# Six 0/1 patterns built on GpSimd, and a mean subtracted in one operation, in a gated window-attention decode step

## The chip, the cores and the metric

The kernel runs on one core of one Trainium2 chip. A core has five engines that run their own instruction streams: TensorE (PE: matrix products), VectorE (DVE: element by element, sums and 32x32 transposes), ScalarE (ACT: functions and copies), GpSimd (POOL) and SyncE (SP, which here only issues transfers). Sixteen DMA engines move data between the chip's memory (HBM) and the on-chip memory SBUF; matrix products go into a third memory, PSUM. Engines wait for each other by semaphores.

The metric is device time in microseconds (us), the median of several runs. The profile is one further execution, recorded by the hardware profiler; its span goes from the first to the last instruction.

## The reference

One decode step, batch 2, one new token, all numbers 32-bit floats. With `xn = layernorm(x)`:

```python
def _A_ref(x, k_cache, v_cache, wq, wo):          # x: [2, 1, 512]
    W = min(4096, max(256, Sk // 4))              # the last 4096 of 32768 positions
    q = heads_of(x @ wq)                          # 32 heads of 128
    k = repeat(k_cache[:, :, Sk - W:, :], 4)      # 8 key heads, each for 4 query heads
    v = repeat(v_cache[:, :, Sk - W:, :], 4)
    p = softmax(q @ k^T * 128 ** -0.5)
    return rows_of(p @ v) @ wo                    # wo: [4096, 512]

def _B_ref(x, w_in, w_sp, b_sp, w_out):           # w_in: [512, 1792], w_out: [896, 512]
    z = gelu(x @ w_in)
    z1, z2 = z[..., :896], layernorm(z[..., 896:])
    g = w_sp * z2 + b_sp
    return (z1 * g) @ w_out

out = x + _A_ref(xn, ...) * silu(_B_ref(xn, ...))
```

## The kernel before, in words

**Data.** A ring of four SBUF slots (`ring`) takes every large load. The loads are queued in this order, all on SyncE's DMA queue: `w_in` (slot 0), `w_out` (slot 1), `wq` (slots 2 and 3), then the units of keys and values, then `wo` in pieces. A unit is the window of two key heads of one batch row, 4096 KB of keys and as much of values; there are eight. Their order is k0, k1, v0, k2, v1, and so on to k7, v6, v7. A load is issued when its slot is free, and `advance` (line 92) is called where the program has finished with a slot. So k0 follows the products of z (slot 0, line 268), k1 the products of y (slot 1, line 321), v0 and k2 the products of q (slots 2 and 3, line 343), v1 the last transpose of k0, and so on.

**Order.** VectorE, ScalarE, TensorE and SyncE are called through a wrapper (`InOrder`, line 27), and execute in the order in which the program is written. GpSimd is called directly; before the change it makes the identity matrix and clears some tiles (lines 184 to 201), all at the start.

**Opening.** VectorE sums the identity into `rowm` (128x32, a one where row mod 32 is the column) and `grpm`, then normalizes x (lines 218 to 227). TensorE turns it, and VectorE copies it into `xnT` (line 231). Then VectorE builds the constant patterns of lines 233 to 257, all from `rowm`, `rowr`, `diag` and `am`, which are sums over columns of `rowm`:
- `same` (128x128, ones where the rows agree mod 32) is the weight of the product `rp`, which adds up the masked q (line 355);
- `same_r` (128x128) is that of the products `mo`, for the maximum and the sum of the softmax (lines 395 and 416);
- `sel` (128x56) selects the rows of a unit in `collect` (line 451), and `place` (128x131) places the heads in `gather` (line 464);
- `add_dq` (128x131) adds the four shares of a score in `add_shares` (line 386);
- `negm` (128x2, 0 or -1e30) is part of the bias of the exponential, `nb` (line 399); `spot` masks the maxima (line 392).

**z and its mean.** When `w_in` is there, 32 products make z (line 264), VectorE transposes it, and works out gelu on 128x28 values. For the layernorm of z's second half, a product with ones sums over the rows, VectorE sums the 7 columns of each batch row into `mean`, and two VectorE operations scale it and subtract it:

```python
mean_over_rows(mean, z2, "mean_ps")
dve.tensor_scalar_mul(mean, mean, 1.0 / FH)
dve.tensor_sub(z2, z2, ap(mean, 0, per_b))
dve.tensor_mul(w2, z2, z2)
mean_over_rows(var, w2, "var_ps")
```

The tile `mean` is later written anew by `rsqrt`. The result goes to `hT`, 14 products with `w_out` make y (line 318), and the gate follows. Then q is made, turned and spread (lines 334 to 358).

**Units.** For each unit, VectorE transposes the keys in four parts (`turn`, tile `kt`), TensorE makes scores (`shares`, `add_shares`), VectorE, TensorE and ScalarE make the softmax of the unit before, and TensorE multiplies it with the values (`values`, tile `acc`). At the end the products with `wo` are added up, multiplied by the gate, added to x and stored (lines 515 to 536).

Of the kernel before, what the change touches and what calls it, by code (L numbers as in the profile page):

```python
# [11 lines left out]
ALU = mybir.AluOpType  # L12
AX = mybir.AxisListType

P = 128
HQ, DH = 32, 128
G = 4
EPS = 1e-5
BIG = 1e30


def ap(t, offset, dims):

    return bass.AP(tensor=t.tensor, offset=t.offset + offset, ap=[list(t.ap[0])] + [list(d) for d in dims])
# [18 lines left out]
def kernel(  # L43
# [13 lines left out]
    nc = tc.nc  # L57
    pe, dve, act, sp = (InOrder(tc, e) for e in (nc.tensor, nc.vector, nc.scalar, nc.sync))
# [5 lines left out]
    FH = F // 2  # L64
# [7 lines left out]
    NCH = J // JC  # L72
# [28 lines left out]
    def const(name, *shape):  # L101
        return cst.tile([P, *shape], F32, tag=name, name=name)
# [92 lines left out]
    sel = const("sel", 56)  # L195
    nc.gpsimd.memset(sel, 0.0)
    place = const("place", 3 + P)
# [5 lines left out]
    rowm = const("rowm", 32)  # L203
# [27 lines left out]
    dve.tensor_copy(xnT[:, :, :B], pt)  # L231

    same = const("same", G, 32)
    dve.tensor_copy(same, ap(rowm, 0, [[0, G], [1, 32]]))
    same = same.rearrange("p g c -> p (g c)")
    rowr = const("rowr", 8)
    dve.tensor_reduce(rowr, rowm.rearrange("p (r m) -> p r m", m=NCH), axis=AX.X, op=ALU.add)
    same_r = const("same_r", G, 8, NCH)
    dve.tensor_copy(same_r, ap(rowr, 0, [[0, G], [1, 8], [0, NCH]]))
    same_r = same_r.rearrange("p g r m -> p (g r m)")  # L240
    diag = const("diag", NCH)
    dve.tensor_reduce(diag, rowm.rearrange("p (r m) -> p m r", m=NCH), axis=AX.X, op=ALU.add)
    dve.tensor_copy(sel[:, 24:32], rowr)
    dve.tensor_copy(place[:, 3 : 3 + P : 4], rowm)
    for a in range(2):
        dve.tensor_copy(
            ap(add_dq, NCH - 1 + 16 * a, [[32, G], [4, REP]]),
            rowm[:, 16 * a : 16 * a + 16].rearrange("p (g h) -> p g h", g=G),
        )
    am = const("am", 2)  # L250
    dve.tensor_reduce(am, rowm.rearrange("p (a x) -> p a x", a=2), axis=AX.X, op=ALU.add)
    negm = const("negm", 2)
    dve.tensor_scalar(negm, am, -1.0, BIG, op0=ALU.add, op1=ALU.mult)
    spot = const("spot", 2, G, NCH)
    for a in range(2):
        dve.tensor_mul(spot[:, a], ap(grpm, 0, [[1, G], [0, NCH]]), ap(diag, 0, [[0, G], [1, NCH]]))
# [33 lines left out]
    z1, z2, w2 = zT[:, 0], zT[:, 1], uu[:, 0]  # L290
    mean, var = const("mean", B), const("var", B)

    def mean_over_rows(dst, src, name):
        pm = bank(name, "mo")[:, : FT * B]
        pe.matmul(pm, ones, src.rearrange("p j b -> p (j b)"), start=True, stop=True)
        dve.reduce_sum(dst, pm.rearrange("p (j b) -> p b j", b=B), axis=AX.X)

    per_b = [[0, FT], [1, B]]
    mean_over_rows(mean, z2, "mean_ps")
    dve.tensor_scalar_mul(mean, mean, 1.0 / FH)  # L300
    dve.tensor_sub(z2, z2, ap(mean, 0, per_b))
    dve.tensor_mul(w2, z2, z2)
    mean_over_rows(var, w2, "var_ps")
    dve.tensor_scalar(var, var, 1.0 / FH, EPS, op0=ALU.mult, op1=ALU.add)
# [260 lines left out]
```

## Time and profile before

| | before |
|---|---|
| median of 3 runs | 218.9 us (218.65 to 219.15) |
| the profiled execution's own time | 218.71 us |
| its span | 216.9 us |
| VectorE instructions, busy | 176, 108.5 us |
| GpSimd instructions, busy | 14, 2.6 us |
| TensorE matrix products, busy | 866, 153.2 us |
| read from HBM | 89.40 MB |

How to read it: a row of the timeline is the start in us, the duration in us, the engine, the line of the code, the operation, the tile written, `<-`, the tiles read, their shapes, and how many instructions are merged in the row. In square brackets stands how long the engine stood idle before, and what ended that. All operations that go through the wrapper carry the wrapper's line, L37, so they are told apart by their tiles. `SPq` is SyncE's queue: its rows are issues of transfers. A row of the windows gives, for a stretch A:B of the span, its length, then the busy time of each engine with the number of instructions, the granted clock of TensorE, the mean busy share of the sixteen DMA engines, and GB/s. A row of the groups gives the busy time of all instructions of one kind, and after the comma the mean of one in ns. The chain of waits goes back from the last instruction to what released it, again and again. Packets and matrix products are recorded with modelled ends, so that in a short stretch a share can be over 1.

### The profile page before, as it was taken

To read this page: it belongs to the slowest core of one execution; us is meant where nothing else is said; L and a number is where in the kernel's file an instruction comes from. 1 tells how busy PE (TensorE), PEld (TensorE's weight loads), DVE (VectorE), ACT (ScalarE), POOL (GpSimd) and SP (SyncE) were. 2 spreads that over 40 slices of the span, in tenths; PEclk is the share of its full clock that TensorE was granted. 3 is DMA by queue.
4 is the path that set the end of the run, shared out by engine and by line. 5 is a ranking of instruction groups with operands and counts; after the bars stand their busy time and mean duration, and the time that the engine had idled before them with its cause. 6 is when DMAs were issued, how large, how long until landed. Compare 5 with 4: busy or idle time off the path is not lost.

```text
span 216.9 us, 2230 instructions
## 1 busy us (share of the span) xinstructions
PE 153.2 (71%) x866; PEld 42.9 (20%) x866; DVE 108.5 (50%) x176; ACT 44.0 (20%) x109; POOL 2.6 (1%) x14
## 2 busy tenths in 40 slices
PE   0173163943987995994997698469959958997761
PEld 0121110200221221221221121322212211232210
DVE  2505411069959369538806942594578089321001
ACT  4003310000222133042113203120421331242010
POOL 4000000000000000000000000000000000000000
PEclk9997575896796997998599799857996996999997
DMA  7998897999999999999999999999999999999980
GB/s 255 423 532 387 387 545 320 468 393 477 393 459 411 447 420 441 429 417 447 405 452 411 453 411 450 417 441 429 429 435 432 435 417 441 417 444 411 407 321 3
DMA packets 3790, 89.54 MB, mean 413 GB/s; under 512 B 434, under 2 KB 450, under 8 KB 964
## 3 DMA queue, kind: packets, MB, share of 16 engines
q1 hardware_dynamic: 3772, 89.40, 96.3%
q8 instruction: 7, 0.11, 0.2%
q14 instruction: 3, 0.02, 0.0%
q10 hardware_dynamic: 8, 0.00, 0.0%
HBM read 89.40 MB, written 0.00 MB: 412 GB/s over the span
## 4 chain that ended last, share of the span: by engine, by line
DMA 70%; PE 17%; DVE 10%; issue 1%; SPq 0%; DVEq 0%
DMA ring<-in_A_k_cache_dram 34%; DMA ring<-in_A_wo_dram 20%; DMA ring<-in_A_wq_dram 16%; DVE kt L37 8%; PE q_ps L37 4%; PE acc L37 4%; PE sh L37 4%; PE s L37 3%; PE mo L37 1%; PE oT L37 0%; PE col L37 0%; SPq L37 0%; DVE res L37 0%; DVE pT L37 0%; DVE m L37 0%
## 5 line engine op out<-in xcount | busy, mean ns | idle before, releaser
L37 DVE STREAM_TRANSPOSE kt<-ring 128x2048 f32<-128x2048 f32 x32 | 72.5, 2294 | 35.6 <-DMA ring<-in_A_k_cache_dram 25.8
L37 PE MATMUL sh<-kt,qbd 128*32 128x512 f32 x256 | 41.8, 706 | 14.8 <-DVE kt L37 14.8
L37 ACT ACTIVATE shs<-sh 128x512 f32<-128x512 f32 x32 | 19.1, 597 | 119.6 <-PE sh L37 119.6
L37 PE MATMUL s<-shs,add_dq 128*128 128x512 f32 x64 | 40.7, 742 | 0.0
L37 PE MATMUL acc<-ring,pT 128*32 128x512 f32 x256 | 31.9, 639 | 0.2 <-DVE pT L37 0.2
L37 PEld LDWEIGHTS s<-shs,add_dq 128*128 128x128 f32 x64 | 11.2, 218 | 29.9 <-issue 25.5
L37 PEld LDWEIGHTS sh<-kt,qbd 128*32 128x32 f32 x256 | 6.6, 113 | 34.6 <-issue 21.0
L37 PEld LDWEIGHTS acc<-ring,pT 128*32 128x32 f32 x256 | 7.7, 117 | 26.1 <-issue 18.3
L37 PE MATMUL q_ps<-ring,xnT 128*32 128x512 f32 x64 | 8.9, 721 | 4.8 <-DMA ring<-in_A_wq_dram 4.8
L37 PE MATMUL mo<-l,same_r 128*128 128x2 f32 x16 | 3.3, 274 | 10.6 <-ACT p L37 10.6
L37 ACT ACTIVATE o<-acc,wd 128x128 f32<-128x128 f32 x32 | 9.1, 373 | 3.4 <-PE acc L37 3.4
L37 ACT ACTIVATE p<-s,nb 128x256 f32<-128x256 f32 x16 | 7.6, 489 | 7.2 <-DVE nb L37 6.9
L37 PE MATMUL part<-ring,oT 128*32 128x512 f32 x56 | 6.6, 597 | 3.3 <-DMA ring<-in_A_wo_dram 3.3
L37 DVE TENSOR_REDUCE m<-s 128x2 f32<-128x512 f32 x8 | 5.4, 676 | 6.8 <-PE s L37 6.8
L37 PE MATMUL col<-o,sel 128*32 128x512 f32 x16 | 8.3, 601 | 0.4 <-ACT o L37 0.4
L37 PE MATMUL z<-ring,xnT 128*32 128x448 f32 x32 | 5.1, 810 | 4.2 <-DMA ring<-in_B_w_in_dram 4.2
L37 DVE STREAM_TRANSPOSE qT<-q_ps 128x512 f32<-128x512 f32 x2 | 1.4, 717 | 10.8 <-PE q_ps L37 10.7
L37 DVE TENSOR_TENSOR res<-so,gate 128x128 f32<-128x128 f32 x1 | 0.3, 292 | 11.7 <-PE so L37 11.7
L37 DVE STREAM_TRANSPOSE pT<-p 128x512 f32<-128x512 f32 x8 | 5.4, 673 | 1.2 <-ACT p L37 1.2
L37 PE MATMUL y<-ring,hT 128*32 128x512 f32 x14 | 3.2, 969 | 3.8 <-issue 3.8
L37 PE MATMUL xnT_ps<-ident,xn 2*128 2x2 f32 x4 | 0.6, 252 | 7.3 <-DVE xn L37 7.3
L37 ACT ACT_TABLE_LOAD x4 | 5.1, 1283 | 1.9 <-issue 1.9
(106 smaller groups left out, 64.4 us busy)
## 6 DMA issues: line engine op xcount, KB each, us to landing
ring<-in_A_k_cache_dram SPq DMA_DIRECT2D x8, 4096.0 KB, 28.2
ring<-in_A_v_cache_dram SPq DMA_DIRECT2D x8, 4096.0 KB, 30.8
ring<-in_A_wo_dram SPq DMA_DIRECT2D x1, 4096.0 KB, 33.2
ring<-in_B_w_in_dram SPq DMA_DIRECT2D x1, 3584.0 KB, 11.2
ring<-in_A_wo_dram SPq DMA_DIRECT2D x1, 2048.0 KB, 27.4
ring<-in_B_w_out_dram SPq DMA_DIRECT2D x1, 1792.0 KB, 15.1
ring<-in_A_wo_dram SPq DMA_DIRECT2D x1, 1024.0 KB
ring<-in_A_wo_dram SPq DMA_DIRECT2D x4, 256.0 KB, 17.5
```

The lines of the kernel that those rows point to most:

```text
L37: return self.tc.keep_in_program_order(call(*args, **kwargs))
```

## The change

Seven VectorE instructions that build six patterns (`same`, `same_r`, `sel`, `place`, `add_dq` in two halves, `negm`) are issued on GpSimd. The sums over columns that they read (`rowm`, `rowr`, `am`), and `diag` and `spot`, stay on VectorE. GpSimd also clears `sel`, `place` and `add_dq`, as before. In z's layernorm, the scaling of the sum and the subtraction become one operation, z2 = sum x (-1/896) + z2; the tile `mean` then holds the sum until `rsqrt` writes it.

```diff
     same = const("same", G, 32)
-    dve.tensor_copy(same, ap(rowm, 0, [[0, G], [1, 32]]))
+    nc.gpsimd.tensor_copy(same, ap(rowm, 0, [[0, G], [1, 32]]))
...
-    dve.tensor_copy(same_r, ap(rowr, 0, [[0, G], [1, 8], [0, NCH]]))
+    nc.gpsimd.tensor_copy(same_r, ap(rowr, 0, [[0, G], [1, 8], [0, NCH]]))
...
-    dve.tensor_copy(sel[:, 24:32], rowr)
-    dve.tensor_copy(place[:, 3 : 3 + P : 4], rowm)
+    nc.gpsimd.tensor_copy(sel[:, 24:32], rowr)
+    nc.gpsimd.tensor_copy(place[:, 3 : 3 + P : 4], rowm)
     for a in range(2):
-        dve.tensor_copy(
+        nc.gpsimd.tensor_copy(
             ap(add_dq, NCH - 1 + 16 * a, [[32, G], [4, REP]]),
...
-    dve.tensor_scalar(negm, am, -1.0, BIG, op0=ALU.add, op1=ALU.mult)
+    nc.gpsimd.tensor_scalar(negm, am, -1.0, BIG, op0=ALU.add, op1=ALU.mult)
...
     mean_over_rows(mean, z2, "mean_ps")
-    dve.tensor_scalar_mul(mean, mean, 1.0 / FH)
-    dve.tensor_sub(z2, z2, ap(mean, 0, per_b))
+    dve.scalar_tensor_tensor(z2, ap(mean, 0, per_b), -1.0 / FH, z2, op0=ALU.mult, op1=ALU.add)
     dve.tensor_mul(w2, z2, z2)
```

## The prediction

> **What bounds the kernel now.** I read the first page from the top: the span, the busy shares, then the DMA queue and the chain.
>
> ```profile
> span 216.9 us, 2230 instructions
> PE 153.2 (71%) x866; PEld 42.9 (20%) x866; DVE 108.5 (50%) x176; ACT 44.0 (20%) x109; POOL 2.6 (1%) x14
> ...
> q1 hardware_dynamic: 3772, 89.40, 96.3%
> ...
> DMA 70%; PE 17%; DVE 10%; issue 1%; SPq 0%; DVEq 0%
> ```
>
> VectorE is busy half of the span, GpSimd 1%, and one DMA queue 96.3%: 89.40 MB pass through it. The chain of waits gives DMA 70% and still leaves 10% to VectorE and 17% to TensorE. Those two shares say that some load was issued only when VectorE or TensorE had freed its slot. They do not say that the DMA engines stood idle until then. That is a question for the stretches of time, for which I ended each stretch at an issue of SyncE's queue.
>
> ```profile
> core 0: us, PE busy (x) PEld busy (x) DVE busy (x) ACT busy (x) POOL busy (x), PEclk, DMA share, GB/s
> 1.60:30.30 28.70, 10.45 (x56) 3.99 (x56) 9.51 (x48) 6.72 (x11) 1.58 (x6) 0.82 1.06 446
> 1.60:58.60 57.00, 26.76 (x157) 7.72 (x157) 24.55 (x71) 8.81 (x14) 1.58 (x6) 0.79 1.00 427
> 1.60:72.40 70.80, 37.94 (x208) 10.75 (x212) 35.76 (x83) 12.22 (x22) 1.58 (x6) 0.81 1.01 432
> 1.60:202.30 200.70, 144.90 (x770) 40.26 (x770) 107.72 (x174) 43.40 (x108) 1.58 (x6) 0.86 1.00 430
> 1.60:212.30 210.70, 152.82 (x858) 42.74 (x858) 107.72 (x174) 43.99 (x109) 1.58 (x6) 0.86 0.99 425
> ```
>
> The share of the 16 DMA engines is 0.99 to 1.06 in all of them. Now the issues, and their sizes from the page:
>
> ```profile
> 1.62 0.48 SPq L37 DMA_DIRECT2D ring<-in_A_wq_dram  x1
> 17.30 13.53 SPq L37 DMA_DIRECT2D ring<-in_A_k_cache_dram  x2
> 41.71 0.54 SPq L37 DMA_DIRECT2D ring<-in_A_v_cache_dram  x1
> 45.14 0.54 SPq L37 DMA_DIRECT2D ring<-in_A_k_cache_dram  x1
> 58.60 0.54 SPq L37 DMA_DIRECT2D ring<-in_A_v_cache_dram  x1
> 72.39 0.54 SPq L37 DMA_DIRECT2D ring<-in_A_k_cache_dram  x1
> ...
> ring<-in_A_k_cache_dram SPq DMA_DIRECT2D x8, 4096.0 KB, 28.2
> ...
> ring<-in_B_w_in_dram SPq DMA_DIRECT2D x1, 3584.0 KB, 11.2
> ...
> ring<-in_B_w_out_dram SPq DMA_DIRECT2D x1, 1792.0 KB, 15.1
> ...
> ring<-in_A_wq_dram SPq DMA_DIRECT2D x1, 34.5
> ```
>
> From these I work out what was still on its way when a load was issued. The second key load, the other of the pair at 17.30, ends its issue at 30.83, and as one issue takes 0.54 us it begins at 30.3. Issued before it: w_in 3.67 MB, w_out 1.84, wq 8.39 (512 x 4096 floats; issued at 1.62 behind the two others), the first key unit 4.19 (a value unit is as large), together 18.09 MB. Moved by then: 446 GB/s x 28.7 us = 12.80 MB. So 5.29 MB waited, or 12 us of transfer at 430 GB/s. At 58.60 it is 30.67 less 24.34, 6.3 MB or 14.7 us; at 72.39 it is 34.87 less 30.59, 4.3 MB or 10 us. At 202.30, the last issue of the loads, 89.14 less 86.30 leaves 2.8 MB or 6.6 us. The queue serves in order of issue: wq is the third load, its mark is 13.9 MB, 446 GB/s reaches that at about 32.8 us, and it is seen to land at 1.62 + 34.5 = 36.1, some 3 us later; had the key unit issued at 17.30 shared the engines evenly with it, both would have ended near the mark of 18.09 MB, some 9 us later. So the kernel is a stream of 89.4 MB, with a short lead before it and a short tail behind it, and work on the engines costs time only if it holds up an issue by more than 6 to 15 us.
>
> **The change part by part.** The first group of moved instructions, and the join, on VectorE; then what waits for the result:
>
> ```profile
> 8.04 0.22 DVE L37 COPY same<-rowm 128x128 f32<-128x128 f32 x1
> 8.17 0.18 DVE L37 TENSOR_REDUCE rowr<-rowm 128x8 f32<-128x32 f32 x1
> 8.38 0.23 DVE L37 COPY same_r<-rowr 128x128 f32<-128x128 f32 x1
> ...
> 9.17 0.17 DVE L37 TENSOR_SCALAR negm<-am 128x2 f32<-128x2 f32 x1
> ...
> 9.80 0.23 DVE L37 TENSOR_SCALAR spot<-spot,am 128x16 f32<-128x16 f32 x1
> 17.59 0.16 DVE L37 COPY wb<-wb_ps 128x2 f32<-128x2 f32 x1 [7.56 <-PE wb_ps L37]
> ...
> 21.91 0.17 DVE L37 TENSOR_SCALAR mean<-mean 128x2 f32<-128x2 f32 x1
> 22.11 0.17 DVE L37 TENSOR_TENSOR zT<-zT,mean 128x14 f32<-128x14 f32 x1
> 22.32 0.17 DVE L37 TENSOR_TENSOR u<-zT 128x14 f32<-128x14 f32 x1
> ...
> 12.11 5.13 PE L37 MATMUL z<-ring,xnT 128*32 128x448 f32 x32 [4.19 <-DMA ring<-in_B_w_in_dram]
> ...
> 27.03 3.21 PE L37 MATMUL y<-ring,hT 128*32 128x512 f32 x14 [3.81 <-issue]
> ...
> 47.41 0.67 PE L37 MATMUL rp<-qm,same 128*128 128x256 f32 x2 [2.33 <-DVE qm L37]
> ```
>
> *Off VectorE.* Seven instructions leave (same, same_r, sel, place, two of add_dq, negm), between 8.04 and 9.25. The run of 14 instructions in which they stand goes from 8.04 to 10.03, 1.99 us or 0.14 each; seven are about 1.0 us. VectorE then stands idle for 7.56 us until z's matmuls are done, and these start at 12.11 when w_in lands. The gain there is nothing; its cover is that idle time.
>
> *On to GpSimd.* The same seven, behind fourteen memsets. Its nearest rows:
>
> ```profile
> masks.py:199 POOL TENSOR_SCALAR_AFFINE_SELECT ident<-ident 128x128 f32<-128x128 f32 x1 | 0.3, 292 | 0.0
> ...
> 2.23 0.95 POOL L201 MEMSET oT<- 128x1024 f32 x1
> ```
>
> No copy on GpSimd is in this trace. The select reads and writes 128x128, the shape of `same` and `same_r`: I take 0.29 us for each of the seven, 2.0 in all. Its bounds are VectorE's own 0.17 to 0.23 below (1.2 to 1.6 for seven) and the 0.95 of the memset of 1024 columns above, 6.7 for seven. GpSimd is through with its memsets at about 3.2 (2.23 + 0.95), so `same` runs there; the six others wait, in order, for `rowr`, which moves up by 0.13 and ends at about 8.2. They end at 10, by the upper bound at 13.9. The first reader is the matmul of `rp` at 47.41, released by `qm`; the others read later. So 33 us of cover, and 14.7 us more in the queue at 58.60. Nothing stands behind these seven on GpSimd, and it issues no DMA, so no transfer is moved past another. Cost zero; VectorE also loses its waits for GpSimd's memsets of sel, place and add_dq, done by 3.2, worth zero.
>
> *New waits.* TensorE (rp, the sums over add_dq, same_r, sel, place) and VectorE (nb) now wait once each for GpSimd, for something long done. That costs an entry in the sequencer, between 0 and the 0.06 of an "issue" piece of the chain at its start:
>
> ```profile
> 0.67 0.06 issue
> ```
>
> Six such are at most 0.4 us over the whole kernel, all behind the queue's 10 us. I take zero on the end.
>
> *The join.* Scaling `mean` and subtracting take 22.32 - 21.91 = 0.41 us. One scalar_tensor_tensor takes their place. Nearest row, the same operation with another shape:
>
> ```profile
> L37 DVE SCALAR_TENSOR_TENSOR nb<-mx,negm 128x2 f32<-128x2 f32 x8 | 1.3, 160 | 0.3
> ```
>
> 0.16, and the tensor subtract of 128x14 takes 0.17; with the 0.03 between instructions 0.20. So 0.21 us goes; at worst, if the form costs the 0.23 of the 128x128 copy of `same_r`, 0.15. This is on the path of its own stage: w2, var, the two activations, hT and y all move up, so y starts at 26.8 instead of 27.03 and the second key load is issued at 30.1. There 5.3 MB are queued ahead of it, so it starts to move when it did. The gain is 0; if the queue had been dry, 0.21.
>
> *Tail.* The end is set by the last piece of wo, from 202.30:
>
> ```profile
> 202.30 9.96 DMA ring<-in_A_wo_dram
> ...
> 212.30 0.47 PE so L37 x8
> ```
>
> No line of this is touched. Sum: 0 us on the span of 216.9. The profiled execution took 218.71 us, 1.8 outside the span and 0.19 under the median of the three runs, 218.9; what the change leaves alone keeps that difference, so I forecast 218.9.
>
> **The rivals.**
> *The early gain reaches the end.* If VectorE and not the stream set the pace, 0.21 and the 1.0 of the seven would show: 218.9 - 1.2 = 217.7. For it: the chain's 10% VectorE. Against it: z is released by w_in with 4.19 us of idle TensorE before it, and the DMA share of 1.00. The join alone would give 218.7, within what can be told apart: I call 0.2% (0.44 us) the least that a measurement here shows, since the runs of one program lie from 218.65 to 219.15.
>
> [...]
>
> [...]
>
> *The stream itself runs at another rate (slower, or faster).* Place: the long middle. Price, from stretches of 20 us:
>
> ```profile
> 80.00:100.00 20.00, 16.27 (x86) 4.27 (x81) 12.09 (x18) 5.21 (x14) 0.00 (x0) 0.91 0.99 424
> 100.00:120.00 20.00, 16.13 (x78) 4.03 (x78) 11.83 (x14) 5.02 (x15) 0.00 (x0) 0.83 1.02 435
> ```
>
> 20 us at 424 instead of 430 GB/s cost 0.28 us; three such stretches make 219.7, and three at 435 save 0.7 and make 218.2. It decides from 0.9 GB/s (0.2%) over the whole stream. For it: the neighbours here differ by 2.6% and the program's code and issue times change a little. Against it: 89.4 MB in the same order and the same packets, and the ups and downs cancel in the runs before.
>
> [...]
>
> **How the numbers follow.** No change within 0.2%: 0.70, at 218.9, own range 218.5 to 219.3. Faster by over 0.2%: 0.15, of which 0.03 the early gain and 0.12 a faster stream (218.2). Slower by over 0.2%: 0.15, of which 0.13 a slower stream (219.7) and 0.02 the blocking (219.9). The range goes from 218.1, just under the faster stream, to 219.8, just over the slower one, and leaves out the early gain and the blocking in full and a tail of the stream's, together about 0.1.
>
> **What would show it.** GpSimd with 21 instructions, the last six ending near 10 us; VectorE with 168; z's matmuls still at 12.1 behind w_in; y at 26.8, the second key load at 30.1; wq still landing at 36.1, the third key load still issued at 45.1, and the last piece of wo at 212.3. If the load at 45.1 moves by more than 0.2 us, or if the last load lands early or late with all else in place, the reading of an in-order, never empty stream is wrong, or its rate has shifted. A `same` that ends after 47 us would break the cover.

## The result, and the profile after

The changed kernel takes 218.12 us (median of 14 runs, 217.37 to 218.63) against 218.71 (14 runs, 218.31 to 219.31): a ratio of 0.9968, 95% interval 0.9957 to 0.9979. That is 0.6 us faster; the forecast was no change. The changed kernel's profiled execution took 217.37 us, its fastest run, so the profile shows somewhat more than the medians do.

The page after, first the span and the busy shares, then the DMA queues and the chain:

```profile
span 215.6 us, 2230 instructions
PE 156.5 (73%) x866; PEld 43.6 (20%) x866; DVE 107.5 (50%) x168; ACT 44.0 (20%) x109; POOL 3.9 (2%) x21
...
q1 hardware_dynamic: 3772, 89.40, 97.0%
q8 instruction: 7, 0.11, 0.2%
q14 instruction: 2, 0.02, 0.0%
...
DMA 48%; PE 34%; DVE 15%; issue 1%; SPq 0%; DVEq 0%
```

VectorE has eight instructions fewer and GpSimd seven more, as written. The large queue carries the same packets. A line that the prediction left unread differs: the queue q14, of the kind that the page calls instruction, has 2 packets in the span. On the page of before it reads:

```profile
q8 instruction: 7, 0.11, 0.2%
q14 instruction: 3, 0.02, 0.0%
```

I take the packets of these queues for fetches of instructions: by that name, and because the last packet on q14 comes earlier or later with the number of VectorE's instructions (216.53 us with 193 of them, 182.25 with 198; the experiments below).

The stream and the timeline of SyncE's queue and of the engines after:

```profile
1.60:30.30 28.70, 10.24 (x53) 4.00 (x56) 8.59 (x40) 6.71 (x10) 2.90 (x13) 0.84 1.05 443
1.60:202.30 200.70, 147.09 (x774) 40.93 (x778) 106.81 (x166) 43.44 (x108) 2.90 (x13) 0.85 1.00 429
1.60:212.30 210.70, 156.44 (x866) 43.64 (x866) 106.81 (x166) 44.04 (x109) 2.90 (x13) 0.85 0.99 425
```

```profile
18.23 13.70 SPq L37 DMA_DIRECT2D ring<-in_A_k_cache_dram  x2
...
45.83 0.53 SPq L37 DMA_DIRECT2D ring<-in_A_k_cache_dram  x1
...
73.79 0.54 SPq L37 DMA_DIRECT2D ring<-in_A_k_cache_dram  x1
...
213.07 0.60 SPq L37 DMA_DIRECT2D out_dram<-res  x1
```

```profile
3.14 0.29 POOL L234 COPY same<-rowm 128x128 f32<-128x128 f32 x1
...
8.10 0.21 POOL L253 TENSOR_SCALAR negm<-am 128x2 f32<-128x2 f32 x1
...
12.56 5.61 PE L37 MATMUL z<-ring,xnT 128*32 128x448 f32 x32 [5.33 <-DMA ring<-in_B_w_in_dram]
...
22.83 0.17 DVE L37 SCALAR_TENSOR_TENSOR zT<-mean,zT 128x14 f32<-128x14 f32 x1
23.04 0.17 DVE L37 TENSOR_TENSOR u<-zT 128x14 f32<-128x14 f32 x1
...
27.77 3.55 PE L37 MATMUL y<-ring,hT 128*32 128x512 f32 x14 [3.84 <-DVE hT L37]
```

In this execution w_in landed half a microsecond later and z's products took 5.61 us for 5.13, so the loads of keys were issued 0.7 to 1.4 us later than before (45.83 for 45.14, 73.79 for 72.39). The stream moved the same 425 GB/s up to 212.3 all the same, and its end did not follow: the end of the chain after is

```profile
201.94 9.95 DMA ring<-in_A_wo_dram
...
211.94 0.47 PE so L37 x8
...
212.43 0.30 DVE res L37
```

so the last load landed at 211.89 where it had been 212.26. That is 0.37 of the 1.3 us between the spans. The other 0.93 us lie behind the output's issue, at 213.44 before and 213.07 after. What SyncE's queue waited for at the very end, before and then after:

```profile
SPq L560 <- DMA out_dram<-res: 1.7, 1, 1.7
```

```profile
SPq L559 <- DMA out_dram<-res: 0.7, 1, 0.7
```

The output is 4 KB in both. The DMA view of one microsecond at that place, in slices of 25 ns, shows what else was on the engines, before (214.3 to 215.3) and after (213.9 to 214.9):

```profile
GB/s 0 0 0 0 0 0 0 0 0 0 0 328 0 0 0 20 61 41 0 0 0 0 0 0 0 0 0 0 0 0 0 0 0 20 20 0 0 0 0 0
...
q14 instruction: 1, 0.01, 3.6%
q1 hardware_dynamic: 12, 0.00, 1.6%
```

```profile
GB/s 0 0 0 0 0 0 0 0 0 0 0 0 0 0 0 0 20 61 62 21 0 0 0 0 0 0 0 0 0 0 0 0 0 0 0 0 0 0 0 0
...
q1 hardware_dynamic: 12, 0.00, 1.6%
```

Bytes are counted where a packet begins (8192 bytes in a slice of 25 ns are the 328 GB/s). After, the eight packets of the output begin within 0.1 us. Before, a packet of 8192 bytes on q14 begins at 214.58, and of the output's eight packets six begin at 214.68 to 214.73 and the last two at 215.15 and 215.17; the q14 packet lasts 569 ns, to 215.15. So two of the output's packets began when a fetch of instructions ended. My guess is a DMA engine that the fetch and these two shared; which engine a packet is on is not in the trace.

The trace also holds four times at which parts of the output, two packets each, were reported to SyncE as landed: before at 215.10, 215.10, 215.11 and 216.10, after at 214.69, 214.71, 214.71 and 214.75. SyncE goes on 0.02 us behind the last of them. So one part in four is late, by a microsecond, and the three others are not.

### The profile page after: what moved, and what is told of

Its sections match the earlier page's. It is cut to its first block, busy times and chain, and to the rows that moved or that the text cites. A ratio compares the mean times of both kernels' runs of the same rounds, so it can differ in the third digit from the quotient of the medians.

```text
span 215.6 us, 2230 instructions
## 1 busy us (share of the span) xinstructions
PE 156.5 (73%) x866; PEld 43.6 (20%) x866; DVE 107.5 (50%) x168; ACT 44.0 (20%) x109; POOL 3.9 (2%) x21
## 3 DMA queue, kind: packets, MB, share of 16 engines
q1 hardware_dynamic: 3772, 89.40, 97.0%
## 4 chain that ended last, share of the span: by engine, by line
DMA 48%; PE 34%; DVE 15%; issue 1%; SPq 0%; DVEq 0%
DMA ring<-in_A_wo_dram 20%; DMA ring<-in_A_wq_dram 16%; DMA ring<-in_A_k_cache_dram 12%; DVE kt L37 10%; PE s L37 10%; PE sh L37 9%; PE acc L37 7%; PE q_ps L37 4%; PE col L37 1%; PE mo L37 1%; DVE qm L37 1%; DVE qbd L37 1%; DVE m L37 1%; PE rp L37 1%; PE oT L37 0%
## 5 line engine op out<-in xcount | busy, mean ns | idle before, releaser
L37 PE MATMUL sh<-kt,qbd 128*32 128x512 f32 x256 | 43.4, 727 | 14.0 <-DVE kt L37 14.0
L37 PE MATMUL acc<-ring,pT 128*32 128x512 f32 x256 | 30.3, 612 | 0.2 <-DVE pT L37 0.2
L37 PE MATMUL q_ps<-ring,xnT 128*32 128x512 f32 x64 | 9.6, 770 | 3.6 <-DMA ring<-in_A_wq_dram 3.6
L37 PE MATMUL z<-ring,xnT 128*32 128x448 f32 x32 | 5.6, 875 | 5.3 <-DMA ring<-in_B_w_in_dram 5.3
L37 PE MATMUL part<-ring,oT 128*32 128x512 f32 x56 | 7.9, 714 | 1.1 <-DMA ring<-in_A_wo_dram 1.1
L37 PEld LDWEIGHTS mo<-l,same_r 128*128 128x128 f32 x16 | 3.0, 233 | 12.2 <-ACT p L37 12.2
```

What stands on the lines that cost most here:

```text
L37: return self.tc.keep_in_program_order(call(*args, **kwargs))
```

## The experiments

Three theories, and a rival that came up on the way. **F**: the length of VectorE's program decides when its last 8192 bytes of instructions are fetched; in the kernel before this falls beside the output's transfer, and that is the gain. **M**: the moved work and the joined operation shorten the path. **S**: the stream of loads became shorter. **L**, the rival: each VectorE instruction costs some time. Below, a program's length is the number of VectorE instructions that the trace records, waits and drains included: 194 before, 187 after (the page counts neither waits nor drains, and the changed program has one wait more). Ratios are against runs of the kernel before on the same chip.

**Seven idle copies added to the changed kernel.** Length 194 again (175 operations by the page's count, as with the join alone below; but one wait more than there).

```diff
     for a in range(2):
         dve.tensor_mul(spot[:, a], ap(grpm, 0, [[1, G], [0, NCH]]), ap(diag, 0, [[0, G], [1, NCH]]))
         dve.tensor_scalar_mul(spot[:, a], spot[:, a], am[:, a : a + 1])
+    scratch = const("scratch", NCH)
+    for _ in range(7):
+        dve.tensor_copy(scratch, diag)
```

> The changed kernel, plus seven VectorE copies of 128x4 into a tile that nobody reads, in the idle time before z (VectorE has 175 operations, one less than before; GpSimd 21 as after the change). Theory F (a fetch of VectorE's instructions, 8192 bytes on the queue q14, falls beside the output's transfer at the end when VectorE's program is long): the third q14 packet is back after 213 us, the wait of SyncE's queue for the output is back near 1.7 us, and the time is about 0.5 us over the changed kernel, 0.1 under before. Theory M (what counts is that the patterns are built on GpSimd or that one operation of the mean is gone): the time stays 0.6 us under before. Theory S (the stream of loads got shorter by itself): the last load lands near 211.9 whatever the tail does, and the time is 0.4 under before.

218.70 us against 218.85: 0.9996 (0.9985 to 1.0007). The whole gain is gone, with all six patterns still on GpSimd and the mean still joined. Its waits, and its DMA view from 214.3 to 215.3:

```profile
SPq L562 <- DMA out_dram<-res: 1.6, 1, 1.6
```

```profile
GB/s 0 0 0 0 0 0 0 0 0 0 328 0 0 0 61 61 0 0 0 0 0 0 0 0 0 0 0 0 0 0 20 20 0 0 0 0 0 0 0 0
...
q14 instruction: 1, 0.01, 3.2%
```

The picture of before is back: the fetch, six packets, and two that are late. Theory M falls.

**Nothing of the change, but a shorter program.** Length 186. The kernel leaves out the four operations that refine a reciprocal root; the function that holds them is called twice.

```diff
     act.activation(dst, t, AF.Exp, scale=-0.5)
-    dve.tensor_mul(t, dst, dst)
-    dve.tensor_mul(t, t, a)
-    dve.tensor_scalar(t, t, -0.5, 1.5, op0=ALU.mult, op1=ALU.add)
-    dve.tensor_mul(dst, dst, t)
```

> The kernel before with GpSimd as it was and both means as they were, but without the four VectorE operations that refine each of the two reciprocal roots, so VectorE's program is eight shorter; the refinement is left out of the result. Theory F: no q14 packet at the end, the wait for the output near 0.7 us, time about 0.6 us under before, although nothing of the change is in it. Theory M: the time of before, since nothing was moved to GpSimd and the 0.8 us that z's chain is shorter by is behind the queue of loads. Theory S: the time of before, within 0.2 us.

217.82 us against 218.85: 0.9962 (0.9949 to 0.9974), the gain of the change without any of it.

```profile
SPq L556 <- DMA out_dram<-res: 0.8, 1, 0.8
```

**The two parts alone.** The join (length 193), and the seven moved instructions (188). Each takes from the diff of the change its own lines.

```diff
-    dve.tensor_scalar_mul(mean, mean, 1.0 / FH)
-    dve.tensor_sub(z2, z2, ap(mean, 0, per_b))
+    dve.scalar_tensor_tensor(z2, ap(mean, 0, per_b), -1.0 / FH, z2, op0=ALU.mult, op1=ALU.add)
```

> The join of the mean alone: VectorE's program one shorter, GpSimd as before. Theory F: the time goes with the q14 packet: with the packet at the end 0.0 to 0.1 us under before, without it 0.6 under. Theory M (the early 0.21 us of z's chain reaches the end): 0.2 us under before. My prediction's reading: 0.

> The seven moved instructions alone, the mean in two operations as before: VectorE's program seven shorter. Theory F: no q14 packet at the end, 0.6 us under before, as the whole change. Theory M by the moved work on VectorE: the whole change less the 0.2 of the join, 0.4 under before. My prediction's reading: 0.

The join alone: 218.14 us, 0.9972 (0.9961 to 0.9982). The move alone: 217.92, 0.9965 (0.9952 to 0.9979). Each part alone brings the whole gain, so the two do not add up; what they share is a shorter program. One instruction is enough. In the join's profile the fetch has not gone: it comes after the output, at 216.53, the only transfer between 216 and 217 us, and the wait is short. That is behind the span, which ends at 216.2; the page counts only what begins inside it, so two packets on q14 there do not mean that the third is never fetched. The trace of the move has it at 217.74; the traces of the change and of the run without the refinement show none.

```profile
SPq L559 <- DMA out_dram<-res: 0.8, 1, 0.8
```

```profile
GB/s 0 0 0 0 0 0 0 0 0 0 0 0 0 0 0 0 0 0 0 0 0 328 0 0 0 0 0 0 0 0 0 0 0 0 0 0 0 0 0 0
...
q14 instruction: 1, 0.01, 2.5%
```

**Six copies for seven.** Length 193, one less than in the first experiment.

```diff
-    for _ in range(7):
+    for _ in range(6):
```

> As the run with seven added copies, but with six: VectorE's program is one shorter than there (193 of its instructions recorded, as with the join alone; 194 with seven and in the kernel before). Theory F: the step lies between these two, so no fetch falls beside the output, the wait for the output is near 0.8 us and the time 0.6 us under before. A theory by which each VectorE instruction costs a little (0.6 us over seven, 0.09 each): 0.1 us under before.

218.19 us against 218.89: 0.9969 (0.9956 to 0.9981), the wait 0.8 us. One copy of 128x4 in an idle stretch at 8 us is worth half a microsecond at the end (218.70 and 218.19, each beside its own runs of before). A cost of each instruction, theory L, would have given 0.1.

**A longer program.** The kernel before with four, two and one of the idle copies (lengths 198, 196, 195).

```diff
+    scratch = const("scratch", NCH)
+    for _ in range(4):      # 2, 1 in the two others
+        dve.tensor_copy(scratch, diag)
```

> The kernel before with four copies of 128x4 added on VectorE in the idle time before z: nothing moved, nothing joined, the program four longer. Theory F: the fetch is asked for four instructions earlier, while VectorE waits for the last products (201 to 212 us), so it falls into the stream of loads and not beside the output; the wait for the output is near 0.8 us and the time 0.6 us under before, although the program is longer. Theory L (a longer VectorE program costs, by its length): the time of before or 0.1 to 0.4 us over it.

> The kernel before with two such copies. Theory F: the fetch is asked for two instructions earlier, near VectorE's last two operations at 212.8 to 213.1, so it falls between 212 and 214.3, ahead of the output's packets at 214.6: time 0.3 to 0.6 us under before. Should it still overlap with them, the time is that of before and the wait near 1.7 us. Theory L: the time of before.

> The kernel before with one copy of 128x4 added on VectorE in the idle time before z. With two added the fetch came at 213.6, a microsecond ahead of the output's packets; in the kernel before it came at 214.58, a tenth of a microsecond ahead of them. Theory F: one instruction moves the request by at most one of VectorE's last operations (about 0.3 us), so the fetch comes between 213.9 and 214.5; it lasts 0.3 to 0.6 us, so it ends before the packets or overlaps with their first. Time between that of before and 0.6 us under it, by whether the wait for the output is near 1.7 or near 0.8 us. Theory L (length): the time of before.

| kernel | length | the fetch begins | output's packets begin | wait for the output | ratio (95%) |
|---|---|---|---|---|---|
| before + 4 | 198 | 182.25 | 214.95 to 215.04 | 0.8 us | 0.9955 (0.9937 to 0.9973) |
| before + 2 | 196 | 213.62 | 214.50 to 214.59 | 0.8 us | 0.9963 (0.9948 to 0.9979) |
| before + 1 | 195 | 213.77 | 214.48 to 214.56 | 1.1 us | 0.9975 (0.9964 to 0.9985) |
| before | 194 | 214.58 | 214.68 to 215.17 | 1.7 us | 1 |
| change + 7 copies | 194 | 214.56 | 214.65 to 215.09 | 1.6 us | 0.9996 (0.9985 to 1.0007) |
| the join | 193 | 216.53 | 214.63 to 214.71 | 0.8 us | 0.9972 (0.9961 to 0.9982) |

Adding instructions makes the kernel before faster by as much as taking them away does. With two added, the fetch is ahead of the output (view from 213.3 to 214.8, slices of 37 ns):

```profile
GB/s 0 0 0 0 0 0 0 0 218 0 0 0 0 0 0 0 0 0 0 0 0 0 0 0 0 0 0 0 0 0 0 0 55 41 14 0 0 0 0 0
...
q14 instruction: 1, 0.01, 1.7%
```

With four it is in the stream of loads, but at 182 us and not at 201 to 212 as expected (view from 182 to 183):

```profile
q1 hardware_dynamic: 12, 0.36, 87.8%
q14 instruction: 1, 0.01, 2.0%
```

So where in the program the fetch is asked for is not simply one instruction per instruction; that stays open. With one added, the fetch ends at 214.31, before the output's first packet, and the packets come together; still the wait is 1.1 us, between the two others. Again it is one part of the output alone: three are reported at 214.91 to 214.92, the fourth at 215.25.

```profile
SPq L563 <- DMA out_dram<-res: 1.1, 1, 1.1
```

**The same for TensorE's last fetch.** The last packet on q8, 16384 bytes, begins at 211.26 us before and at 211.29 after, beside the last packets of the loads; I take it for a fetch of TensorE's. The changed kernel, with a longer program on TensorE:

```diff
+    early = bank("early", "mo")[:, :2]
+    for _ in range(12):
+        pe.matmul(early, ones, ones[:, :2], start=True, stop=True)
     pt = bank("xnT_ps", "sh")[:, : KT * B]
```

> The changed kernel with twelve products of ones by ones (128x2) added on TensorE in its idle time at the start, so that TensorE's own fetch of 16384 bytes (the last packet of the queue q8, at 211.3 us, beside the last packets of the loads) is asked for some 48 instructions earlier, near 206 to 208 us. If a fetch on a busy DMA engine costs the end its own length, the last load lands up to 0.4 us earlier or not at all, as the engines share the same bytes: by the first 217.7, by the second the time of the changed kernel, 218.1.

217.88 us against 218.53: 0.9972 (0.9960 to 0.9983), the ratio of the change itself. The fetch moved to 210.2 only, not to 206 to 208, so the first alternative had no full trial; no gain is seen.

None of these kernels is faster than the changed one beyond the intervals.

## Why the prediction was wrong, point by point

- **The stream bounds the kernel, and the engines' early work is hidden: right.** After, y and the key loads were 0.7 to 1.4 us later than before, and the last load landed 0.4 us earlier. The prediction's sign of being wrong, the load of 45.1 moved by more than 0.2 us, did appear (45.83): `wq` still landed at 36.1, but q's products took 9.70 us for 8.98. The sign was too strict. In the eleven profiles this load is issued between 44.48 and 46.59, and the stream moves 425 GB/s up to 212.3 in each. In the ten profiles taken after the prediction, the first of VectorE's two operations that make the result starts between 212.38 and 213.07, with no order by what the kernel saves or adds at the start.
- **Seven instructions off VectorE gain nothing by themselves, the join gains 0.2 us in its stage and nothing at the end: right as work.** From the operation that reads `mean` to the square it is 23.04 - 22.83 = 0.21 for 0.41. With the patterns on GpSimd and the mean joined, and the program brought back to its length, the time is that of before (0.9996).
- **GpSimd has 33 us of cover: right.** Its seven instructions take 0.19 to 0.29 us each and end at 8.3, before the 10 forecast; 0.7 us of that is x, which landed earlier in this execution. They do not run in the written order: those that read `rowm` go first, and did not wait for `rowr` as forecast. No operation that reads a pattern waits for GpSimd in the trace.
- **VectorE held up by GpSimd (the blocking, 0.02 at 219.9): no run shows the microsecond of it.** What the trace of the changed kernel shows is one longer operation. VectorE's first `spot` product took 229 ns beside GpSimd's copy of `same_r` (7.59 to 7.88), where both took 168 to 170 before. The second, which began at 8.09, just ahead of GpSimd's `negm`, took 168:

```profile
L37 DVE TENSOR_TENSOR spot<-grpm,diag x2: 168/198/229, 7.7 to 8.1; 128x16 f32<-128x16 f32 x2
```

  That is 0.06 us, ahead of 10.00 us in which VectorE stands idle until z's products are done. The other VectorE operations beside GpSimd's seven took as long as before: `mv` and `va` (beside `same`) 0.17 and 0.14 us, the sums `diag` and `am` 0.20 and 0.18, the two products `spot`<-`spot`,`am` 234 ns each. Why the one product was longer is not shown.
- **The step that failed: the tail.** "No line of this is touched. Sum: 0 us." The lines of the tail are untouched, but its transfers are not alone. The page of before had the row that speaks of it, q14 with 3 packets, and the prediction asked what the added and removed instructions do, not what their number moves on that queue. What the runs showed in place of that 0: the wait for the output is 1.7 us with the fetch beside it and 0.7 to 0.8 without, and the time 0.6 us lower. In the list of rivals "the program's code and issue times change a little" stood as a reason for another rate of the stream; the code's length was what the gain turned on, in another place.
- **The number.** The measured 218.12 lies beside the 218.2 that the prediction gave for a faster stream. That is chance: the stream did not bring it.
- **The rivals.** The early gain at the end (217.7) is refuted by the first experiment. A faster stream isn't needed: of two kernels that differ by one copy, the one with the fetch beside the output takes 218.70 us, the other 218.19. A stream faster by 0.4 us, as in the one profiled execution, does not go with the change: over the ten profiles the last load lands between 211.84 and 212.28, at 211.98 in the kernel with seven copies, which is as slow as before, and at 212.20 and 212.26 in the join and the move, which are as fast as the change.
- **"The end is set by the last piece of wo": not always.** In four of the ten profiles (seven copies, no refinement, before + 1 and + 4) the chain ends through ScalarE's copy `parts` and TensorE's last 24 products instead, and the result starts up to 0.26 us later than the last load alone would let it. It goes neither with the fetch nor with the time.

Two things stay open. The two late packets begin 0.42 us behind the others (215.15 for 214.73), while the wait for the output is 0.8 to 1.0 us longer. The rest lies between the late part's last packet and its report. In the eight kernels with a short wait this takes 0.34 to 0.35 us; it takes 0.90 in the kernel before, 0.80 with seven copies and 0.67 in before + 1, where the packets themselves are not late. Why the report is later is not shown, and how a DMA engine shares a fetch and an output was not tried. That the fetch delays the output is shown by the wait coming and going with it: 1.7 and 1.6 us with the fetch at 214.58 and 214.56, 0.7 to 0.8 with it elsewhere or not in the trace (1.1 in before + 1), and the time with it.

The medians of the kernels with the shorter waits lie 0.6 to 1.0 us under those of before, and the changed kernel is at the low end. Its runs spend 2.08 us outside the span (median of 14), those of the kernel before 1.8 us, and its profile is one of its two runs with 1.8; so in the twelve others a part of the gain is lost outside the span. The move and the run with a longer program on TensorE, which spend 2.0 and 2.1 us there, have the fetch behind the span in their traces, at 217.74 and 217.33. Whether it is the fetch that costs this was not tried.

## What to carry to other kernels

When a stream of loads hides the engines, look at what is left uncovered: the lead and the tail, and there at everything on the DMA engines, the queues of instructions included (10 of the 3790 packets on the page of before). Here an edit that changes only how many instructions VectorE has moved such a fetch on to the last, exposed transfer or away from it: 218.70 us with seven idle copies, 218.19 with six. Before a gain of this size is credited to the work that was saved, add as many idle instructions back and see if it stays. It went the other way too: one idle copy more made the kernel before faster (0.9975), so for a kernel that became half a microsecond slower for no reason one idle instruction more or less is worth a trial.

## What the runs showed of the hardware

- The profile counts packets of the kind instruction among those of the sixteen DMA engines: of the 3790 of before, 3772 are on q1, 8 on q10, 7 on q8 and 3 on q14. In the span those on q14 are 8192 bytes (0.3 to 0.57 us each), and the last of them moves with VectorE's length (182.25 to 216.53 us in the table above); those on q8 are 16384 bytes (0.88 to 1.20 us each, seven in the kernel), and move with TensorE's (the third at 95.4 for 108.7 us with the twelve products more).
- A fetch beside an output of eight 512-byte packets made the wait for that output 1.6 to 1.7 us, where it is 0.7 to 0.8 without. Of the output's four parts only one is late (before, 216.10 us for 215.10 to 215.11).
- The effect is narrow: of the recorded lengths 186, 187, 188, 193, 194, 195, 196 and 198, only 194 has the full cost, in two quite different programs, and 195 a part of the longer wait (1.1 us).
